# ELU output of a fused attention and mixture-of-experts kernel: transposed on VectorE and through DRAM instead of on TensorE

## The chip, the cores and the metric

The kernel runs on one core of one Trainium2 chip. The metric is device time in microseconds (us), the median of several runs; all times in this document are in us unless marked ns. The engines are TensorE (PE; its weight loads stand apart as PEld), VectorE (DVE), ScalarE (ACT), GpSimd (POOL) and SyncE (SP), which here only issues DMAs.

## The reference: what is computed

Three layers in a row, all in fp32 on the inputs of the reference (the first layer's weights arrive as float64 and are narrowed on the chip):

```python
# 1: attention, 8 batches x 8 heads, 576 positions, head size 64, causal by blocks of 64
scores = (q @ k.T) / 8, masked by blocks;  attn = softmax(scores);  x = attn @ v      # x: 4608 x 512
# 2: a dense layer with ELU
h = x @ w_in                                  # 4608 x 2048
g = where(h > 0, h, exp(min(h, 0)) - 1)
x2 = g @ w_out                                # 4608 x 512
# 3: soft mixture of experts: 8 experts, 4 slots each
logits = x2 @ phi                             # 4608 x 32
d = softmax(logits over tokens);  slot_input = d.T @ x2
slot_out[e] = relu(slot_input[e] @ w1[e]) @ w2[e]    # w1, w2: 16 MB each
out = softmax(logits over slots) @ slot_out          # 4608 x 512
```

x2 itself is never formed: the kernel folds `w_out @ phi` into one matrix of 2048 x 32 (`WP`), takes the logits as `g @ WP`, and gathers `d.T @ g` over all tokens before it multiplies by `w_out`.

## The kernel before

**Tiling.** The 4608 tokens are 36 tiles of 128. The 64 heads are 32 pairs of heads, four pairs to a batch. For each tile the first layer is done in four *ranges* of 512 of the 2048 columns. In one range TensorE runs 12 matmuls of 128x512 (lines 613 to 615: high by high, high by low, low by high parts, four steps over the 512 inputs) into one of two PSUM banks; ACT takes the exponential (L618); DVE forms min(e,1)-1 (L620) and then max(e,h) (L623), which is `g` of 128 tokens x 512 columns, put into one of the `NG` = 6 slots of the buffer `G`.

**The part that is changed.** The logits need `g` turned, with its 2048 columns on the partitions. So after each range `gtr` in `tile_range` turns it on TensorE in four 128x128 transposes (all transposes go by the helper on L312) into the PSUM bank `GTB`, and ACT or DVE copies that bank into `GT` (L288 or L290). `tile_logits` then multiplies each range by its 512 rows of `WP` (L636: four matmuls, recorded as eight, with 32 stationary and 128 moving columns; four column groups side by side). When all four ranges are in, `tile_dispatch` does the two softmaxes' steps (L648 to L676) and `d.T @ g` (L686), and adds that to a running sum (L690).

**Attention** uses the same engines between the ranges: block scores (L474, L478), row maxima and exponentials (L487, L490), normalisation on POOL (L507), 26 transposes a pair on TensorE (also L312), their copies (L288, L290), and the products with v (L573, L581). Its q and k are loaded in stripes of 32 partitions with runs of 128 bytes and turned by DVE (L443).

**Order.** The kernel is one static program. Each step is an operation with an engine, an estimated duration and a key; `Plan.order` simulates the engines and takes, on each of them, the operation with the lowest key among those whose inputs are ready by its estimate (for a DMA: issue, 0.65, bytes at 360 GB/s, and 1.0 more). Every engine, SP's queue too, runs its list in that order and waits at the head where an input is late. Tile i has key 22 i; the last attention pair is keyed at tile 30.

**Head and end.** Until some 160 us the float64 weights are loaded, narrowed and split while the first pairs of heads run. The expert weights and `w_out` (36 pieces of 1 MB, `piece` and `quarters` in `tail`, lines 749 and 763) have no buffers of their own: 24 slots become free one after the other, 12 in the attention's buffers, two in the ring `XR`, eight in the first layer's weights (two to a range), one in `XH`/`XL` and one in `GT`. The last two tiles run range by range together (`last_tiles`). After them come `slot_input` (L806), the experts (L827, L849), two rounds of four experts each, and the output (L916).

Of the kernel before, what the change touches and what calls it, by code (L numbers as in the profile page):

```python
# [27 lines left out]
NEV, NQ = 16, 1  # L28
TICK, DUTY, FILL, FN = 3.4, 0.5, 0.055, 128
# [21 lines left out]
class Plan:  # L51
# [9 lines left out]
    def __init__(self):  # L61
        self.ops = []
        self.writers = {}
        self.readers = {}
        self.fills = []
        self.load = {}

# [5 lines left out]
    def add(self, engs, dur, fn, r=(), w=(), key=0.0, nbytes=0, load=1.0):  # L73
# [17 lines left out]
        self.load[i] = load  # L91
        return i

    def order(self):
# [32 lines left out]
        while events:  # L127
            now = events[0][0]
            while events and events[0][0] <= now + 1e-9:
                _, kind, i = heapq.heappop(events)  # L130
                if kind == 0:
                    for e in self.ops[i][0]:
                        heapq.heappush(heaps[e], (self.ops[i][4], i))
            for e in engines:
                if free[e] > now + 1e-9:
                    continue
                h = heaps[e]
                while h and done[h[0][1]]:
# [12 lines left out]
                _, i = heapq.heappop(h)  # L151
                done[i] = True
                engs, dur, fn, deps, key, nbytes = self.ops[i]
                d = dur[engs.index(e)]
                busy[e] += d
                free[e] = now + d
                fin = now + d
                if nbytes:
                    dma_free = max(dma_free, fin + 0.65) + nbytes / 360e3
                    fin = dma_free + 1.0  # L160
                finish[i] = fin
                if e == "PE":
                    recent.append((now, now + d, self.load[i]))
                seq.append((now, i, e))
                heapq.heappush(events, (free[e], 1, -1))
                if fin > free[e] or any(f_[2] == i for f_ in self.fills):
                    heapq.heappush(events, (fin, 1, -1))
                for o in out[i]:
                    hop = 0.0 if nbytes else self.HOPS.get((e, self.ops[o][0][0]), 0.0 if self.ops[o][0][0] == e else 0.15)
                    ready_at[o] = max(ready_at[o], fin + hop)  # L170
                    missing[o] -= 1
                    if not missing[o]:
                        release(o)
# [24 lines left out]
def attention_moe_kernel(ctx: ExitStack, tc, q, k, v, w_in, w_out, phi, w1, w2, consts, out):  # L198
# [18 lines left out]
    SM = base.take(160)  # L217
# [14 lines left out]
    PW = 3200  # L232
    PB = aa.take(2 * PW)
    PAD = aa.take(12 * PIECE - aa.size)
# [16 lines left out]
    wo_f32 = dpool.tile([FF, DM], F32, name="wo_f32")  # L251
    successors = {}
# [52 lines left out]
    def load(o, i, nbytes, r=(), w=(), key=0.0, eng="SP"):  # L305
# [3 lines left out]
        add(engs, tuple(0.48 if x == "SP" else 0.67 for x in engs), fn, r, w, key, nbytes)  # L309
# [11 lines left out]


    def start():
# [3 lines left out]
        def init(e):  # L327
            nc.vector.memset(f(ACC, 512), 0.0)
            nc.vector.memset(f(SM, 160), 0.0)
            nc.vector.memset(f(sum_col, 20), 1.0)  # L330
            nc.vector.memset(f(NMX, 2), 1e30)
# [3 lines left out]
        def zero(e):  # L335
            for s in range(2):
                nc.gpsimd.memset(f(PB + PW * s + S, 64), 0.0)
            for s in range(NV):
                nc.gpsimd.memset(f(V + 640 * s, 640, 64, P).rearrange("p (h x) -> p h x", h=2)[:, :, 256:320], 0.0)
# [6 lines left out]
               [(GT + 1024 * j, 512, [("gt", 2 * j), ("gt", 2 * j + 1)]) for j in range(2)] + \  # L346
# [60 lines left out]
        def give_back():  # L407
# [3 lines left out]
            handover(["c"], [("wot", 0), ("wot", 1)])  # L411
            handover([("e", 0), ("e", 1)] + [("xr", p, 1, j) for p in range(2) for j in range(2)], [("stage", 5)])
# [42 lines left out]

    def wide(x):
        return S if x == "b" else P * (x[0] + 1)

    def pair_scores(n, fill, key):
# [25 lines left out]
        for x in units:  # L485
# [5 lines left out]
                f(PB + PW * s + UNITS[x][1], wide(x)), pb(at(x), wide(x)), AF.Exp, bias=f(c, 1), scale=1.0,  # L491
                accum_out=f(sum_col + 9 * s + UNITS[x][0], 1)),
                r=keys(x) + [("nm", s, x)], w=[("p", x, s), ("sum", s, fill // 2)], key=key)

    def pair_weights(n, half, key):
# [9 lines left out]
        for x in units:  # L505
            p = PB + PW * s + UNITS[x][1]
            add("POOL", 0.2 + wide(x) / 1050, lambda e, x=x, p=p: nc.gpsimd.tensor_scalar(  # L507
                out=f(p, wide(x)), in0=f(p, wide(x)), scalar1=f(rs_col + 9 * s + UNITS[x][0], 1), scalar2=0.0,
                op0=ALU.mult, op1=ALU.add), r=[("rs", s, half)], w=[("p", x, s)], key=key)
# [26 lines left out]
        for gi, (blocks, outs) in enumerate(groups):  # L536
            tb, tk = (POST, "post") if gi % 2 and n < NPB else (PTB, "ptb")

            def tr(e, blocks=blocks, tb=tb):
                for j, (x, c) in enumerate(blocks):  # L540
                    transpose(pb(tb + P * j, P), f(PB + PW * s + UNITS[x][1] + P * c, P))
            add("PE", 0.02 + 0.108 * len(blocks), tr, r=[("p", x, s) for x in {b[0]: 0 for b in blocks}] + ["con"], w=[tk], key=key, load=0.0)
# [20 lines left out]
    def pair_values(n, key):  # L563
# [7 lines left out]
        def first(e):  # L571
            for h in range(2):
                mm(pb(PTB, 64, 64 * h, 64 * h + 64), lhsT=f(vs + 320 * h, D), rhs=f(pts[h], 64), start=True, stop=True)  # L573
        add("PE", 0.17, first, r=rd, w=["ptb"], key=key, load=0.25)
        add(*evict(n, 64), lambda e: copy(e, f(XR + RING * p + ring, 64), pb(PTB, 64)), r=["ptb"], w=[("xr", p, b % 2, 0)], key=key)
        for c in range(5):
            q0 = max(64, P * c)

            def pv(e, c=c, q0=q0):
# [3 lines left out]
            add("PE", 0.02 + (S - q0) / 603, pv, r=rd, w=["pvb"], key=key, load=0.25)  # L583
# [5 lines left out]
    tslot = [(GT + 512 * j, ("gt", j)) for j in range(4)]  # L589
# [15 lines left out]
    def tile_range(i, r, hb, gs, ts, kr):  # L605
        s = i % 2
        xh, xl = XH + 512 * s, XL + 512 * s
        (g, gk), (gt, tk) = gs, ts
# [17 lines left out]

        def gtr(e):
# [3 lines left out]
        add(CP2, cpdur(512), lambda e: copy(e, f(gt, 512), pb(GTB, 512)), r=["gtb"], w=[tk], key=kr)  # L631

    def tile_logits(r, ts, bank, bk, kp):
# [4 lines left out]
        add("PE", 0.3, lg, r=["wp", ts[1]], w=[bk], key=kp, load=0.25)  # L638
# [55 lines left out]
    def moe_tile(i, key):  # L694
        gs = [gslot[(4 * i + r) % NG] for r in range(4)]
        tile_split(i, key - 6)
        for r in range(4):
            tile_range(i, r, r % 2, gs[r], tslot[r], key + 5.5 * r)
        for r in range(4):
            tile_logits(r, tslot[r], POST, "post", key + 17)  # L700
        tile_dispatch([i], [gs], [(POST, "post")], [(LPS, "lps")], (DTX, "dtx"), (DX, "dx"), key + 17)

    def last_tiles(i, key):

        order = [gslot[(4 * i + j) % NG] for j in range(NG)] + tslot[2:]
# [13 lines left out]
    def tail(key):  # L719
        att = [(nm, s, a) for nm in ("rq", "rk") for s in range(2) for a in range(4)] + [(nm, s) for nm in ("qt", "kt") for s in range(2)] + \  # L720
              [("v", s, j) for s in range(NV) for j in range(3)] + [("p", x, s) for x in UNITS for s in range(2)] + \
# [15 lines left out]
        slots += [(held("xhl", 0), hk), (lambda: f(GT, PIECE).rearrange("p (c d) -> p c d", d=512), [("gt", r) for r in range(4)])]  # L737
        for j, (_, olds) in enumerate(slots):
            handover([("piece", j, c) for c in range(4)], olds)
        turn = 2 * list(range(len(slots)))  # L740

        def piece(src, kp, r=()):
# [8 lines left out]
            add("SP", 0.48, fn, r, pkeys(j), kp, 1 << 20)  # L751
# [104 lines left out]
        def late(x, n, dtype, p0=0, p1=P):  # L856
            nm = "w3" if x < 2 * PIECE else "xhl"
# [4 lines left out]
        for m in range(9):  # L862
            handover([("cpkh", m)], sum((pkeys(j) for j in ((20, 21) if m < 8 else (22,))), []))
        handover([("sop", 0), ("sop", 1)], pkeys(22))
# [38 lines left out]
        places = [p1[1, g][1] for g in range(4)] + [23]  # L903
# [79 lines left out]
```

## Time and profile before

| | us |
|---|---|
| median of 3 runs | 1084.82 (1082.36 to 1086.9) |
| the profiled execution's own time | 1082.45 |
| its span, first to last instruction | 1080.7 |
| PE busy | 1034.6 (96%) |
| DVE busy | 617.5 (57%) |
| ACT busy | 499.5 (46%) |
| POOL busy | 275.6 (26%) |

Matmuls are pipelined, so the duration of one (its mean in ns) is longer than the time from one to the next; the chain of waits, which gives each piece of time to one instruction only, shows the latter. In the chain's rows the numbers are the start, the time that the piece adds, the engine, the tensor, the line and the count of instructions. In a table of stretches an engine's number is its busy time, with the count of instructions in brackets; the last three columns are the granted TensorE clock as a share of the full one, the mean busy share of the 16 DMA engines, and GB/s.

### The profile page before, as it was taken

To read this page: it belongs to the slowest core of one execution; us is meant where nothing else is said; L and a number is where in the kernel's file an instruction comes from. 1 tells how busy PE (TensorE), PEld (TensorE's weight loads), DVE (VectorE), ACT (ScalarE), POOL (GpSimd) and SP (SyncE) were. 2 spreads that over 40 slices of the span, in tenths; PEclk is the share of its full clock that TensorE was granted. 3 is DMA by queue.
4 is the path that set the end of the run, shared out by engine and by line. 5 is a ranking of instruction groups with operands and counts; after the bars stand their busy time and mean duration, and the time that the engine had idled before them with its cause. 6 is when DMAs were issued, how large, how long until landed. Compare 5 with 4: busy or idle time off the path is not lost.

```text
span 1080.7 us, 19505 instructions
## 1 busy us (share of the span) xinstructions
PE 1034.6 (96%) x7287; PEld 687.0 (64%) x7287; DVE 617.5 (57%) x1560; ACT 499.5 (46%) x1346; POOL 275.6 (26%) x396
## 2 busy tenths in 40 slices
PE   7878999999999999999999999999999999999993
PEld 4546676666666666666666666666766666767441
DVE  6989663455554555565756665656656564453241
ACT  3766453455454545454544534454444443332134
POOL 4886220122222313122323222231222222010000
PEclk9999889999999999999999999999999999999997
DMA  9988940011111111212111111121110024717969
GB/s 188 201 190 189 229 122 12 18 28 35 33 35 34 34 34 30 38 23 39 29 34 33 35 34 34 23 36 29 30 29 12 1 79 147 282 44 277 348 228 350
DMA packets 219486, 97.95 MB, mean 91 GB/s; under 512 B 192512, under 2 KB 192640, under 8 KB 219392
## 3 DMA queue, kind: packets, MB, share of 16 engines
q1 hardware_dynamic: 217616, 96.49, 34.4%
q8 instruction: 57, 0.93, 0.4%
q10 hardware_dynamic: 1776, 0.22, 0.2%
q14 instruction: 37, 0.30, 0.1%
HBM read 83.05 MB, written 13.63 MB: 89 GB/s over the span
## 4 chain that ended last, share of the span: by engine, by line
PE 86%; DMA 4%; DVE 3%; POOL 2%; SPq 1%; issue 1%; ACT 1%; ACTq 0%; DVEq 0%; POOLq 0%
PE ps L312 16%; PE ps L613 14%; PE ps L615 12%; PE ps L614 12%; PE ps L581 7%; PE ps L478 7%; PE ps L636 4%; PE ps L686 3%; PE ps L474 3%; PE ps L849 1%; POOL att L507 1%; PE ps L827 1%; SPq L307 1%; DMA wo_f<-att 1%; DVE att L374 1%; PE ps L652 1%
## 5 line engine op out<-in xcount | busy, mean ns | idle before, releaser
L613 PE MATMUL ps<-w,xhl 128*128 128x512 f32 x576 | 258.1, 448 | 0.0
L507 POOL TENSOR_SCALAR att<-att,base 128x128 f32<-128x128 f32 (+4 forms) x288 | 173.2, 619 | 246.8 <-DVE base L503 231.2
L615 PE MATMUL ps<-w,xhl 128*128 128x512 f32 x576 | 227.2, 394 | 0.4 <-POOL xhl L600 0.4
L614 PE MATMUL ps<-w,xhl 128*128 128x512 f32 x576 | 226.3, 393 | 0.0
L490 ACT ACTIVATE att<-ps,base 128x128 f32<-128x128 f32 (+4 forms) x288 | 157.4, 553 | 98.9 <-DVE base L487 94.6
L288 ACT COPY att<-ps 128x512 f32<-128x512 f32 (+3 forms) x217 | 106.1, 511 | 123.6 <-PE ps L312 119.0
L312 PE MATMUL ps<-base,att 128*128 128x128 f32 x864 | 140.9, 285 | 11.9 <-POOL att L507 7.4
L620 DVE TENSOR_SCALAR xe<-xe 128x512 f32<-128x512 f32 x144 | 67.6, 469 | 146.4 <-ACT xe L618 145.4
L487 DVE TENSOR_REDUCE base<-ps 128x1 f32<-128x128 f32 (+4 forms) x288 | 137.1, 506 | 23.4 <-PE ps L474 14.7
L312 PEld LDWEIGHTS ps<-base,att 128*128 128x128 f32 x864 | 102.4, 146 | 61.3 <-issue 22.7
L613 PEld LDWEIGHTS ps<-w,xhl 128*128 128x128 f32 x576 | 108.7, 189 | 48.9 <-issue 35.6
L618 ACT ACTIVATE xe<-ps 128x512 f32<-128x512 f32 x144 | 86.1, 598 | 88.5 <-PE ps L615 86.6
L615 PEld LDWEIGHTS ps<-w,xhl 128*128 128x128 f32 x576 | 108.2, 188 | 25.6 <-POOL xhl L600 0.9
L614 PEld LDWEIGHTS ps<-w,xhl 128*128 128x128 f32 x576 | 109.4, 190 | 10.1
L600 POOL TENSOR_TENSOR xhl<-xe,xhl 128x512 fp32r<-128x512 f32 x36 | 47.1, 1310 | 221.4 <-ACT xhl L598 187.7
L478 PE MATMUL ps<-att 64*128 64x128 f32 (+3 forms) x512 | 98.7, 478 | 4.8 <-ACT att L490 4.7
L623 DVE TENSOR_TENSOR g<-xe,ps 128x512 f32<-128x512 f32 x144 | 98.0, 680 | 3.3
L581 PE MATMUL ps<-att 128*64 128x512 f32 (+4 forms) x640 | 94.4, 427 | 0.0
L312 PE MATMUL ps<-base,g 128*128 128x128 f32 x592 | 90.3, 275 | 0.1
L288 ACT COPY g<-ps 128x512 f32<-128x512 f32 (+1 forms) x77 | 44.9, 584 | 87.0 <-PE ps L312 86.0
L312 PEld LDWEIGHTS ps<-base,g 128*128 128x128 f32 x592 | 70.1, 141 | 21.6 <-issue 4.9
L290 DVE COPY g<-ps 128x512 f32<-128x512 f32 (+1 forms) x77 | 52.5, 682 | 42.1 <-PE ps L312 41.5
(115 smaller groups left out, 1089.0 us busy)
## 6 DMA issues: line engine op xcount, KB each, us to landing
att<-in_moe_w_dram SPq DMA_DIRECT2D x12, 1024.0 KB, 13.7
att<-in_k_dram SPq DMA_DIRECT2D x127, 72.0 KB, 2.7
att<-in_q_dram SPq DMA_DIRECT2D x126, 72.0 KB, 2.6
att<-in_v_dram SPq DMA_DIRECT2D x64, 128.0 KB, 2.6
g<-in_moe_w_in_dram SPq DMA_DIRECT2D x16, 512.0 KB, 6.4
w_late<-in_moe_w_dram SPq DMA_DIRECT2D x8, 1024.0 KB, 6.6
att<-in_moe_w_dram SPq DMA_DIRECT2D x32, 256.0 KB, 5.8
out_dram<-att SPq DMA_DIRECT2D x16, 512.0 KB, 5.5
```

The source lines that it names most:

```text
L288: nc.scalar.copy(o, i)
L312: mm(o, lhsT=i, rhs=f(IDN + base, n, base, base + n), start=True, stop=True, is_transpose=True)
L478: mm(pb(at((u, h)), P * (u + 1)), lhsT=f(qt + P * u, P, 64 * h, 64 * h + 64), rhs=f(kt, P * (u + 1), 64 * h, 64 * h + 64), start=True, sto ...
L487: add("DVE", 0.08 + wide(x) / 960, lambda e, x=x, c=c: nc.vector.tensor_reduce(out=f(c, 1), in_=pb(at(x), wide(x)), axis=AX.X, op=ALU.max, ...
L490: add("ACT", 0.42 + wide(x) / 1300, lambda e, x=x, c=c: nc.scalar.activation(f(PB + PW * s + UNITS[x][1], wide(x)), pb(at(x), wide(x)), AF ...
L507: add("POOL", 0.2 + wide(x) / 1050, lambda e, x=x, p=p: nc.gpsimd.tensor_scalar(out=f(p, wide(x)), in0=f(p, wide(x)), scalar1=f(rs_col + 9 ...
L581: mm(pb(PVB + q0 - 64, S - q0, 64 * h, 64 * h + 64), lhsT=f(vs + 320 * h + D * c, D), rhs=f(pts[h] + CHS * c + q0, S - q0), start=(c == 0) ...
L613: mm(pb(bank, 512), lhsT=fr(xh + P * kk, P), rhs=hi, start=(kk == 0), stop=False)
L614: mm(pb(bank, 512), lhsT=fr(xh + P * kk, P), rhs=lo, start=False, stop=False)
L615: mm(pb(bank, 512), lhsT=fr(xl + P * kk, P), rhs=hi, start=False, stop=(kk == 3))
L618: add("ACT", 0.48, lambda e: nc.scalar.activation(f(ee, 512), pb(bank, 512), AF.Exp), r=[("h", hb)], w=[("e", hb)], key=kr)
L623: add("DVE", 0.6, lambda e: nc.vector.tensor_tensor(out=f(g, 512), in0=f(ee, 512), in1=pb(bank, 512), op=ALU.max), r=[("e", hb), ("h", hb) ...
```

## The change

For tiles 0 to 33 the transposes on TensorE, the bank `GTB` and the copies to `GT` go. DVE turns `g` by blocks of 32x32 into a new buffer `TT` (four blocks of rows stay where they were, each block turned in itself). For every two ranges (a half tile) SP writes 128 x 1024 words from `TT` to a DRAM tensor, waits for it, and reads it back in four loads of 32 partitions (runs of 1 KB), which puts the blocks in their places in `GT`. The logits of a tile become one operation behind both halves. The last two tiles keep the old way. `NG` becomes 8. The second half of a pair's weights is no longer double buffered (`PB`); attention's transposes alternate between two PSUM banks throughout, since `GTB` is free; the products with v become one operation. Expert weights have 22 slots, in another order, nine of them in the attention's buffers, and the first 12 pieces also wait in threes until the loads of tiles 30, 31, 32 and 33 have landed. The planner counts 2.5 instead of 1.0 behind the new DMAs.

```diff
+TLAG, PACE0, PACE = 2.5, 30, 3
-    NG = 6
+    NG = 8
     G = ga.take(NG * 512)
-    GT = ga.take(2048)
+    GT = ga.take(PIECE)
+    TT = ga.take(PIECE)
+    PAD = TT
-    PW = 3200
-    PB = aa.take(2 * PW)
-    PAD = aa.take(12 * PIECE - aa.size)
+    PW = (1664, 1536)
+    PB = aa.take(2 * PW[0] + PW[1])
...
+    def pat(x, n):
+        return PB + (PW[0] * (n % 2) + UNITS[x][1] if x in HALVES[0] else PW[0] + UNITS[x][1])
...
-            tb, tk = (POST, "post") if gi % 2 and n < NPB else (PTB, "ptb")
+            tb, tk = (PTB, "ptb") if gi % 2 == 0 else (POST, "post") if n < NPB else (GTB, "gtb")
...
     def tile_range(i, r, hb, gs, ts, kr):
...
+        if ts is None:
+
+            hf = r // 2
+            tt = f(TT + 1024 * hf, 1024).rearrange("p (b c j) -> p c b j", b=4, j=32)[:, 4 * (r % 2):4 * (r % 2) + 4]
+            add("DVE", 0.7, lambda e: nc.vector.transpose(out=tt, in_=f(g, 512).rearrange("p (c b i) -> p c b i", c=4, i=32)),
+                r=[gk], w=[("tt", hf, r % 2)], key=kr)
+            return
+
         def gtr(e):
...
+    def tile_turn(i, hf, kp):
+
+        via = turned[hf]
+        load(via, f(TT + 1024 * hf, 1024), 1 << 19, r=[("tt", hf, r) for r in range(2)], w=[("via", hf)], key=kp, lag=TLAG)
+        for b in range(4):
+            load(f(GT + 1024 * hf, 1024, 32 * b, 32 * b + 32).rearrange("i (a x) -> i a x", a=4),
+                 via.rearrange("(a i) (b x) -> b i a x", a=4, b=4)[b], 1 << 17, r=[("via", hf)],
+                 w=[("gt", hf, b)] + ([("turned", i)] if hf and b == 3 else []), key=kp, lag=TLAG)
+
+    def tile_routing(kp):
+        def lg(e):
+            for c in range(16):
+                j = c % 4
+                gt = f(GT + 1024 * (c // 8), 1024).rearrange("p (a c j) -> p c a j", a=4, j=32)[:, c % 8]
+                mm(pb(POST, P, 32 * j, 32 * j + 32), lhsT=f(WP + NS * c, NS), rhs=gt, start=(c < 4), stop=(c >= 12))
+        add("PE", 1.0, lg, r=["wp"] + gtk(0) + gtk(1), w=["post"], key=kp, load=0.25)
...
         for r in range(4):
-            tile_range(i, r, r % 2, gs[r], tslot[r], key + 5.5 * r)
-        for r in range(4):
-            tile_logits(r, tslot[r], POST, "post", key + 17)
+            tile_range(i, r, r % 2, gs[r], None, key + 5.5 * r)
+            if r % 2:
+                tile_turn(i, r // 2, key + 5.5 * r + 0.5)
+        tile_routing(key + 17)
...
-        slots = [(lambda j=j: f(PT + PIECE * j, PIECE).rearrange("p (c d) -> p c d", d=512), att) for j in range(12)]
-        slots += [(ring(hf), xk[hf]) for hf in range(2)]
-        slots += [(held("w%d" % r, j), wk[r]) for r in range(4) for j in range(2)]
...
+        wslot = [(held("w%d" % r, j), wk[r]) for r in range(4) for j in range(2)]
+        slots = [(flat(PT + PIECE * j), att) for j in range(9)]
+        slots += [(flat(TT), [("tt", j, r) for j in range(2) for r in range(2)])]
+        slots += wslot[:2] + [(ring(hf), xk[hf]) for hf in range(2)] + wslot[2:]
+        slots += [(held("xhl", 0), hk), (flat(GT), gtk(0) + gtk(1))]
...
-            add("SP", 0.48, fn, r, pkeys(j), kp, 1 << 20)
+            pieces.append(j)
+            paced = len(pieces) - 1
+            add("SP", 0.48, fn, list(r) + ([("turned", PACE0 + paced // PACE)] if paced // PACE + PACE0 < NTILE - 2 else []), pkeys(j), kp, 1 << 20)
```

## Rows read from the trace of the kernel before

**Rows 1.** The page: busy time of PE and DVE, and the slices.
```profile
PE 1034.6 (96%) x7287; PEld 687.0 (64%) x7287; DVE 617.5 (57%) x1560; ACT 499.5 (46%) x1346; POOL 275.6 (26%) x396
PE   7878999999999999999999999999999999999993
DMA  9988940011111111212111111121110024717969
```

**Rows 2.** The chain of waits from 300 to 400: shares by line.
```profile
by line: PE ps L312 19.4%; PE ps L613 16.9%; PE ps L615 14.4%; PE ps L614 14.3%; PE ps L581 11.0%; PE ps L478 8.3%; PE ps L636 5.1%; PE ps L474 4.5%; PE ps L686 4.0%; PE ps L573 1.1%; PE ps L652 0.9%; PE ps L653 0.6%
```

**Rows 3.** The chain from 938 to 956: one tile without attention.
```profile
938.42 0.99 PE ps L686 x8
...
940.31 0.44 PE ps L312 x4
...
945.33 0.57 PE ps L636 x16
945.90 0.43 PE ps L613
...
949.17 0.23 PE ps L613
...
949.87 0.36 PE ps L636 x8
...
954.90 0.99 PE ps L686 x8
```

**Rows 4.** Instructions of two TensorE lines; first and last start in us.
```profile
L312 PE MATMUL ps<-base,g 128*128 128x128 f32 x592 | 90.3, 275 | 0.1
L686 PE MATMUL ps<-g,base x272: 592/605/618, 172.8 to 971.8; 128*32 128x512 f32 x136
```

**Rows 5.** DVE and ACT groups, 200 to 880: busy, mean ns; idle time before.
```profile
L620 DVE TENSOR_SCALAR xe<-xe 128x512 f32<-128x512 f32 x109 | 52.0, 477 | 109.4 <-ACT xe L618 108.4
L290 DVE COPY g<-ps 128x512 f32<-128x512 f32 x55 | 37.6, 684 | 14.0 <-PE ps L312 13.4
L443 DVE STREAM_TRANSPOSE att<-att 128x576 f32<-128x576 f32 x46 | 34.8, 762 | 0.9 <-issue 0.8
L623 DVE TENSOR_TENSOR g<-xe,ps 128x512 f32<-128x512 f32 x109 | 74.0, 678 | 2.3
L618 ACT ACTIVATE xe<-ps 128x512 f32<-128x512 f32 x109 | 65.2, 598 | 55.2 <-PE ps L615 53.9
L288 ACT COPY g<-ps 128x512 f32<-128x512 f32 x53 | 31.1, 587 | 41.2 <-PE ps L312 40.8
```

**Rows 6.** DMA issues: count, KB each, median us from issue to landing.
```profile
att<-in_q_dram SPq DMA_DIRECT2D x126, 72.0 KB, 2.6
att<-in_v_dram SPq DMA_DIRECT2D x64, 128.0 KB, 2.6
wo_f<-att SPq DMA_DIRECT2D x16, 256.0 KB, 4.7
out_dram<-att SPq DMA_DIRECT2D x16, 512.0 KB, 5.5
```

**Rows 7.** Stretches: q and k loads alone, and the end's weights.
```profile
416.00:421.00 5.00, 5.00 (x41) 3.53 (x40) 4.07 (x11) 2.12 (x7) 3.66 (x7) 1.00 0.62 101
1010.00:1040.00 30.00, 29.88 (x280) 11.55 (x281) 6.74 (x11) 6.11 (x11) 0.00 (x0) 1.00 1.04 368
```

**Rows 8.** SP's queue: issues of q, 200 to 880 (ns); expert weights in order.
```profile
L307 SPq DMA_DIRECT2D att<-in_q_dram x84: 337/489/1382, 214.1 to 782.9; - x84
...
970.59 24.88 SPq L749 DMA_DIRECT2D w_late<-in_moe_w_dram  x8
...
1021.96 17.84 SPq L763 DMA_DIRECT2D att<-in_moe_w_dram  x16
```

**Rows 9.** The chain from 900 on: the end.
```profile
994.59 0.47 PE ps L636 x8
...
1043.77 2.09 PE ps L849 x7
```

More of the change, by code (lines that the diff above doesn't have):

```diff
@@ L251, in attention_moe_kernel @@
     wo_f32 = dpool.tile([FF, DM], F32, name="wo_f32")
+    turned = [dpool.tile([P, 1024], F32, name="turned%d" % j) for j in range(2)]
     successors = {}
@@ L308, in load @@
         engs = (eng,) if isinstance(eng, str) else eng
-        add(engs, tuple(0.48 if x == "SP" else 0.67 for x in engs), fn, r, w, key, nbytes)
+        add(engs, tuple(0.48 if x == "SP" else 0.67 for x in engs), fn, r, w, key, nbytes, lag=lag)
     def transpose(o, i, n=P, base=0):
@@ L320, in handover, with gtk @@
             plan.readers.setdefault(b, []).extend(sorted(ops))
+    def gtk(hf):
+        return [("gt", hf, b) for b in range(4)]
     def start():
@@ L345, in start @@
         raws = [(G + 1024 * j, 512, [("g", 2 * j), ("g", 2 * j + 1)]) for j in range(3)] + \
-               [(GT + 1024 * j, 512, [("gt", 2 * j), ("gt", 2 * j + 1)]) for j in range(2)] + \
+               [(GT + 1024 * j, 512, gtk(j)) for j in range(2)] + \
                [(XR + 2 * RING + S, RING, [("xr", p, 1, j) for p in (2, 3) for j in range(2)])]
@@ L411, in give_back @@
             handover(["c"], [("wot", 0), ("wot", 1)])
+            handover([("tt", 0, r) for r in range(2)], [("narrow", 0), ("narrow", 1)])
             handover([("e", 0), ("e", 1)] + [("xr", p, 1, j) for p in range(2) for j in range(2)], [("stage", 5)])
@@ L454, in attention_moe_kernel, with pkey @@
     HALVES = (FILLS[0] + FILLS[1], FILLS[2] + FILLS[3])
+    def pat(x, n):
+        return PB + (PW[0] * (n % 2) + UNITS[x][1] if x in HALVES[0] else PW[0] + UNITS[x][1])
+    def pkey(x, n):
+        return ("p", x, n % 2 if x in HALVES[0] else 0)
     def wide(x):
@@ L569, in pair_values, with pv @@
         ring = S * (b % 2)
-        def first(e):
+        def pv(e):
             for h in range(2):
                 mm(pb(PTB, 64, 64 * h, 64 * h + 64), lhsT=f(vs + 320 * h, D), rhs=f(pts[h], 64), start=True, stop=True)
[L574 to L579, printed above, removed]
+            for c in range(5):
+                q0 = max(64, P * c)
                 for h in range(2):
@@ L588, in attention_moe_kernel @@
     gslot = [(G + 512 * j, ("g", j)) for j in range(NG)]
-    tslot = [(GT + 512 * j, ("gt", j)) for j in range(4)]
+    tslot = [(GT + 512 * j, gtk(j // 2)) for j in range(4)]
     def tile_split(i, key):
@@ L720, in tail @@
         att = [(nm, s, a) for nm in ("rq", "rk") for s in range(2) for a in range(4)] + [(nm, s) for nm in ("qt", "kt") for s in range(2)] + \
-              [("v", s, j) for s in range(NV) for j in range(3)] + [("p", x, s) for x in UNITS for s in range(2)] + \
+              [("v", s, j) for s in range(NV) for j in range(3)] + [pkey(x, s) for x in UNITS for s in range(2)] + \
               [x for s in range(NPT) for x in pt_keys[s]]
@@ L733, in ring, with flat @@
             return lambda: f(XR, 4 * RING).rearrange("p (c t) -> p c t", t=RING)[:, :, S * hf:S * hf + 512]
-        slots = [(lambda j=j: f(PT + PIECE * j, PIECE).rearrange("p (c d) -> p c d", d=512), att) for j in range(12)]
-        slots += [(ring(hf), xk[hf]) for hf in range(2)]
-        slots += [(held("w%d" % r, j), wk[r]) for r in range(4) for j in range(2)]
-        slots += [(held("xhl", 0), hk), (lambda: f(GT, PIECE).rearrange("p (c d) -> p c d", d=512), [("gt", r) for r in range(4)])]
+        def flat(o):
+            return lambda: f(o, PIECE).rearrange("p (c d) -> p c d", d=512)
+        wslot = [(held("w%d" % r, j), wk[r]) for r in range(4) for j in range(2)]
[3 more added lines that the diff above has]
+        slots += [(held("xhl", 0), hk), (flat(GT), gtk(0) + gtk(1))]
         for j, (_, olds) in enumerate(slots):
@@ L740, in tail @@
         turn = 2 * list(range(len(slots)))
+        pieces = []
         def piece(src, kp, r=()):
@@ L856, in late @@
         def late(x, n, dtype, p0=0, p1=P):
-            nm = "w3" if x < 2 * PIECE else "xhl"
+            nm = "w2" if x < 2 * PIECE else "xhl"
             t = renew(nm, F32R, 1)
@@ L862, in tail @@
         for m in range(9):
-            handover([("cpkh", m)], sum((pkeys(j) for j in ((20, 21) if m < 8 else (22,))), []))
-        handover([("sop", 0), ("sop", 1)], pkeys(22))
+            handover([("cpkh", m)], sum((pkeys(j) for j in ((16, 17) if m < 8 else (20,))), []))
+        handover([("sop", 0), ("sop", 1)], pkeys(20))
         for s in range(2):
@@ L902, in tail @@
                 op0=ALU.mult, op1=ALU.add), r=[bk[2 * hf], "con"], w=[("sop", hf)], key=ko)
-        places = [p1[1, g][1] for g in range(4)] + [23]
+        places = [p1[1, g][1] for g in range(4)] + [14]
         NO = len(places)
```

37 lines of the change are left out of this document (20 added, 17 removed).

## Prediction

> **What bounds the kernel now.** I read four views: the page's busy times and slices, the chain of waits in the middle, the chain over one late tile, and the end. On the page TensorE is busy for 96% of the span, and from the seventh slice to the last but two it is busy throughout, while VectorE stands at 57% and the DMA engines at one to two tenths [rows 1]. A busy TensorE alone proves little, since durations overlap, so the chain decides: from 300 to 400 every piece of it is a TensorE line, and no wait on another engine or a DMA appears [rows 2]. There the kernel is as long as TensorE's list of work. A change that takes work off that list is worth the time which the chain gives to that work, as long as nothing else becomes late. The period of a tile is (971.8 - 172.8)/33 = 24.2 over the whole run [rows 4] and 954.90 - 938.42 = 16.48 where attention has ended [rows 3]. At the end another limit comes near: from 1010 to 1040 the DMA engines are at a share of 1.04 with 368 GB/s [rows 7], while TensorE is still in the chain.
>
> **What goes: the transposes.** 34 tiles x 4 ranges = 136 groups of four, 544 of the 592 in that row. The profile offers two prices. The mean of one is 275 ns [rows 4], which would make 150; but these overlap, and the chain gives a group of four 0.44 (940.31 to the next matmul) [rows 3]. I take the chain's: 136 x 0.44 = 59.8. The least I can defend is 0.39 a group (where a group stands next to other fp32 work, a part of the switch remains), so 53.
>
> **What goes: blocks of logits.** Matmuls, weights and columns stay the same in number; what changes is that one block of 32 recorded instructions takes the place of several. In the late tile the blocks are 0.57 for 16 and 0.36 for 8 (there are two of 8), 1.29 together; the second eight in a block cost 0.57 - 0.36 = 0.21, so 32 in one block cost 0.36 + 3 x 0.21 = 1.0, a gain of 0.3. Besides, the first matmul of the dense layer after such a block takes 0.43 [rows 3], about 0.2 more than its steady 0.23, and two of three such changes go: 0.4. That is 0.7 for a late tile. In the middle the share of 5.1% of 100 over 4.1 tiles is 1.2 a tile [rows 2], gain 0.2, and a block often stands beside other fp32 work. From 0 to 0.7 x 34 = 24; I take 0.35 x 34 = 12. The moving operand is now read in four runs of 32 words; no row shows that form, and I put its cost at nothing because the columns and their count are the same; were it half as slow again, 0.5 x 34 = 17 would go back.
>
> **What comes on VectorE.** A turn of 128x576 takes 762 ns [rows 5], so 512 columns take about 677: 136 x 0.68 = 92. The copies to `GT` were shared, 55 on DVE at 684 ns and 53 on ACT at 587 in 680 us [rows 5]; of 136 about 69 leave DVE (47) and 67 leave ACT (39). Net DVE gets 45 more, 662 of some 1025, or 65%. Its cover is the wait it has now: before L620 it idles 109.4 for ACT's exponential [rows 5]. I cost this at nothing; without the cover the price would be the 45.
>
> **What comes on the DMA engines.** Each tile writes 1.05 MB and reads 1.05 MB. At 368 GB/s [rows 7] that is 5.7 of a tile's 22, a quarter of the engines, on top of the tenth or two [rows 1]. The writes have 4 KB runs. Reads of 1 KB runs into 32 partitions are not in the trace; the nearest rows are the weights (368 GB/s) and the q and k loads, also 32 partitions but with 128-byte runs: 101 GB/s at a share of 0.62, so 163 at a full one [rows 7]. The reads take 2.9 to 6.4 a tile, nearer the former by their run length. In the middle both fit.
> The Trainium skill says against this form that a DMA into partitions 0 to 31 reaches only half of the SBUF ports and measured 189 GB/s at 1 MiB against 328 for 128 partitions (SBUF — State Buffer, "Door 1: The DMA port swizzle"). By it the reads of a tile would take 5.5, an estimate from that page, and the sum would change only at the end, where the engines are full (the rival on the end below). The row above, 163 at a full share, lies below that page's figure and can't tell it from the cost of short runs.
>
> **What comes on SP.** Ten issues a tile at 0.49 [rows 8] are 5 of 22. But SP waits at the head of its list, for the turn before a write and for the write before the four loads. Behind it stand q, k and v of the next pairs, which are loaded a tile and more ahead, and the next half's write. So it costs nothing while a round trip is a few us.
>
> **The new loop.** Logits now wait for the round trip, and TensorE meanwhile has the next tile's matmuls, up to the point where `G` has no free slot: range 0 of tile i+2 needs the `d.T @ g` of tile i. From the first range of tile i to that point: three ranges, then exponential 0.60, min 0.48, max 0.68, turn 0.68 [rows 5] (2.4), the round trip, logits 1.0, the softmax steps about 5.0 (949.87 to 954.90, with other work of TensorE between) and the product 0.99 [rows 3]. The round trip lies between 2.6 + 2.6 (128 KB loads, not held up) and 5.5 + 5.5 (512 KB in a full stretch) [rows 6]; I take 9. With attention: 16.5 + 2.4 + 9 + 7 = 35 against two periods of 22, 44: 9 to spare, no loss. Without it (tiles 30 on): the period would be 16.48 - 1.76 - 0.7 = 14.0, and 10.5 + 2.4 + 9 + 7 = 29 against 28, so half a us a tile, and more where the paced weights stand in the way. I take +4 for the last six tiles (0 to 10).
>
> **What moves: the expert weights.** Before, 22 pieces had been issued when the dense layer ended at 994.59 + 0.47 (eight of them from 970.59 to 995.5) [rows 8, 9], the last quarters are issued until 1039.8, and the last expert matmuls stand at 1043.77, 49 after the dense layer's end. Now nine pieces go into attention's space behind tiles 30 to 32, and the tenth waits for tile 33, some 11.5 into the 29 of the last two tiles (2.4 + 9), so 17 before the dense layer's end. With the two ring pieces ahead of it 25 are left: 25 x 1.05/0.368 = 71, so they end 54 behind the dense layer instead of 49. In tile 33, 5 pieces and 2.1 MB of turns (7.3 MB, 20 us) would have to fit into 14, so up to 6 more. I take +7 (0 to +15).
>
> **The rest.** Single buffers for half of the pair's weights, a third bank for attention's transposes, merged products, the head with its two moved staging areas: no row shows a gain or a loss. Bounds -5 to +20, taken as +4.
>
> **Sum** against the profiled execution's own 1082.45: -59.8 - 12 + 4 + 7 + 4 = -56.8, so 1025.7. The median of the runs shown is 1084.82, 2.4 above it; on that footing 1028. With the ends: 1084.8 - 60 - 24 - 5 = 996, and 1084.8 - 53 + 17 + 10 + 15 + 20 = 1094, all of them at once.
>
> **Rivals.**
> *The round trip holds TensorE (slower).* Place: the eight slots of `G`. For: each hop is a DMA with a landing time, and SP does them in turn with q, k and v. It decides from a loop of 44 on, a round trip of 18, and makes the kernel slower from a loop of 2 x 24.2 = 48.4, a round trip of 22; at 24, with 25 us a tile, 34 x 0.9 = 30 more than before: 1115. Against: the longest median of a transfer up to 512 KB is 5.5 [rows 6]. Chance 0.07.
> *The end is bound by DMA.* Reads at the q loads' 163 GB/s take 6.4 instead of 2.9, in the last four tiles 14 in all, where the engines have no room; the experts' last pieces are late by as much: 1028 + 14 = 1042, up to 1060. For: the share of 1.04 [rows 7]. Against: it needs all of it to be backlog. The skill's port rule (SBUF — State Buffer, as above) would do the same thing with 4 x 2.6 = 10. Chance 0.18.
> *VectorE sets the pace.* At 65% with more operations between an exponential and the release of a bank it answers late; all 45 of its net work would come back: 1073, half of it: 1050. For: L623 follows L620 at once [rows 5]. Against: 109 us of idle time before L620. Chance 0.08.
> *The turns don't unload TensorE.* The static order puts the logits where the estimate has them, and TensorE waits for what it saved: within 0.5% of 1085. Against: a step of three matmuls takes 3 x 0.23 = 0.69 [rows 3] where the planner counts 0.65, so TensorE runs behind the estimate and inputs come early for it. Chance 0.04.
> *More is saved,* the upper ends of the logits and no stall: 1000 to 1012. Chance 0.08.
>
> **How the numbers follow.** The forecast has 0.55, its own range is 1012 to 1042. With most of the end rival, half of VectorE's and of the larger gain the range is 1008 to 1060. Half a per cent (5.4) is about what a measurement of this kernel can tell from no change. Faster: 0.55 + 0.18 + 0.08 + 0.08 = 0.89; within 0.04; slower 0.07.
>
> **What would show it.** The L312 group from `g` falls from 592 to 48; the chain in the middle stays all TensorE; a late tile lasts about 14, one with attention about 22. The loads from the DRAM tensor land 4 to 5 after issue. DVE has 136 turns at about 0.68 and stands at 65%. From the dense layer's end to the end of the span it takes about 93 instead of 86. Wrong would be: idle time of TensorE before the logits or a chain through DMA in the middle (the loop), a chain through L620 and L623 (VectorE), or more than 65 between the dense layer's end and the last expert matmul (the end).

## The result and the profile after

The changed kernel takes 1044.3 (median of four runs, 1042.8 to 1047.1) against 1084.9: a ratio of 0.963, 95% interval 0.960 to 0.966. The direction was right, the size was not: 56.8 were forecast, 40.6 came. 1044.3 lies inside the wide range (1008 to 1060) and 2 above the forecast's own (1012 to 1042). The profiled execution is the longest of the four (1047.07, span 1045.3, so 35.4 below the span before); the positions below are its.

The page after: busy time, then slices of 26 each.

```profile
PE 973.0 (93%) x6822; PEld 649.2 (62%) x6822; DVE 644.9 (62%) x1603; ACT 465.7 (45%) x1302; POOL 278.5 (27%) x397
...
PE   7879889999999999999999999999999998669993
...
PEclk8989989999999999999999999999999999878996
DMA  9987845454545544545454444544532259875969
```

Against [rows 1], TensorE has lost 62 us of work and VectorE has gained 27. From the seventh slice to the thirty-third TensorE is still busy throughout. What is new stands in slices 34 to 36: an 8 and two 6, with DMA at 9, 8 and 7 and a lower granted clock (8, 7 and 8) in slices 35 to 37. The middle, as the chain of waits from 300 to 400 shows it (share by line; L317 is the old L312, L668 the old L636, L626 to L628 the dense layer):

```profile
by line: PE ps L626 21.0%; PE ps L628 16.4%; PE ps L627 16.4%; PE ps L317 11.1%; PE ps L593 10.4%; PE ps L494 10.0%; PE ps L490 4.5%; PE ps L668 4.0%; PE ps L724 4.0%; PE ps L589 1.1%; PE ps L690 0.9%; PE ps L691 0.6%; issue 0.0%
```

It is all TensorE as in [rows 2]: the transposes' line falls from 19.4% to 11.1%, and the dense layer's three rise from 45.6% to 53.8%, which is what more tiles in the same time look like. The groups of instructions (count | busy, mean ns | idle before), TensorE over the run, then VectorE from 200 to 880; and of the page the new DMAs (count, KB, us to landing):

```profile
L668 PE MATMUL ps<-g,base 128*32 128x128 f32 x1088 | 38.0, 280 | 10.7 <-DMA g<-turned 10.7
L317 PE MATMUL ps<-base,g 128*128 128x128 f32 x112 | 20.8, 315 | 4.4 <-DVE g L382 2.9 <-DVE g L636 1.5
```
```profile
L644 DVE STREAM_TRANSPOSE g<-g 128x512 f32<-128x512 f32 x121 | 83.3, 689 | 1.0
L633 DVE TENSOR_SCALAR xe<-xe 128x512 f32<-128x512 f32 x122 | 57.6, 472 | 75.7 <-ACT xe L631 74.9
```
```profile
turned<-g SPq DMA_DIRECT2D x68, 512.0 KB, 2.8
g<-turned SPq DMA_DIRECT2D x272, 128.0 KB, 3.0
```

The 592 of [rows 4] are 112: 48 of the last two tiles and the end, and 64 of the second layer's weights, whose staging now lies in this buffer. A turn takes 689 ns (677 forecast), and VectorE still waits 75.7 for ScalarE, 109.4 before [rows 5]. The median landing of write and load is 3, nearer the lower bounds of [rows 6].

**Where the gain was lost.** I counted the dense layer's matmuls (its last line, sixteen to a tile) in both traces:

| position | before | after | difference |
|---|---|---|---|
| first of the 31st tile | 892.8 | 832.8 | -60.0 |
| first of the 34th tile | 946.4 | 878.9 | -67.5 |
| last (dense layer's end) | 994.2 | 955.6 | -38.6 |
| end of the span | 1080.7 | 1045.3 | -35.4 |

Up to the 34th tile all that was forecast is there. The last three tiles' matmuls then take 76.7 instead of 47.8, and 29 are lost in that one stretch. Its chain of waits after (start, us, what; SPq and POOLq are the sequencers that issue):

```profile
895.18 0.47 issue
895.65 1.34 POOLq L1023
897.01 0.39 SPq L792
897.44 0.51 SPq L312
...
897.99 7.12 DMA g<-turned
...
914.49 0.43 PE ps L626
914.91 0.43 PE ps L627
...
921.93 0.24 PE ps L628
922.18 0.39 SPq L792
922.62 0.51 SPq L792
...
923.22 0.45 SPq L312
...
925.04 10.37 DMA g<-turned
```

Two things are to be seen. The loads of the turned halves land after 7 and 10 us instead of 3. And ahead of them in SP's list stand pieces of expert weights (L792): one for the ring `XR` at 897.01, which waits for the last use of the ring (on POOL), and two for the first layer's weight buffers at 922.18, which wait for TensorE's matmul of 921.93. SP's own list shows it (start, us from the first to the last issue, count), and below it SP's longest waits from 878 to 956 (who waited for whom: us, times, longest):

```profile
897.01 0.39 SPq L792 DMA_DIRECT2D xe<-in_moe_w_dram  x1
897.44 0.98 SPq L312 DMA_DIRECT2D g<-turned  x2
898.59 0.40 SPq L312 DMA_DIRECT2D turned<-g  x1
899.02 2.18 SPq L792 DMA_DIRECT2D att<-in_moe_w_dram  x3
905.19 0.34 SPq L312 DMA_DIRECT2D turned<-g  x1
906.35 1.76 SPq L312 DMA_DIRECT2D g<-turned  x4
922.18 0.94 SPq L792 DMA_DIRECT2D w_late<-in_moe_w_dram  x2
923.22 2.26 SPq L312 DMA_DIRECT2D g<-turned  x4
```
```profile
SPq L792 <- PE ps L628: 15.4, 2, 13.3
SPq L312 <- DMA turned<-g: 8.4, 2, 7.7
```

The last half was written from 905.19 on, and its four loads are issued at 923.22. Between them TensorE ran matmuls of the last two tiles. The chain gives 0.43 instead of 0.23 to the first 10 of them (0.41 to the next): after TensorE's idle time the granted clock had fallen towards the lower of its two levels, 0.55 in the mean from 910 to 920. Stretches after (the last three numbers: granted clock, DMA share, GB/s), the whole stretch from the 34th tile on among them, and the same work before, 946 to 994.6:

```profile
878.90:956.00 77.10, 57.83 (x342) 39.01 (x340) 22.35 (x50) 14.04 (x35) 2.58 (x2) 0.80 0.73 247
...
910.00:920.00 10.00, 8.53 (x28) 5.57 (x29) 1.94 (x3) 0.57 (x1) 0.00 (x0) 0.55 0.61 208
...
930.00:940.00 10.00, 3.42 (x25) 2.41 (x25) 0.99 (x5) 1.26 (x6) 0.00 (x0) 0.63 1.06 342
```
```profile
946.00:994.60 48.60, 48.57 (x315) 33.94 (x316) 19.94 (x43) 13.63 (x31) 2.71 (x2) 1.00 0.43 149
```

So the 29 have two parts: TensorE idles for 77.1 - 57.8 = 19.3, and it is busy for 57.8 instead of 48.6, 9 more, at a mean clock of 0.80 instead of 1.00. The second is an estimate of what the clock cost, since the two stretches don't hold quite the same instructions (342 and 315).

### The profile page after: what moved, and what is told of

It is laid out like the page before. It is cut to its first block, busy times and chain, and to the rows that moved or that the text cites. A ratio compares the mean times of both kernels' runs of the same rounds, so it can differ in the third digit from the quotient of the medians.

```text
span 1045.3 us, 19077 instructions
## 1 busy us (share of the span) xinstructions
PE 973.0 (93%) x6822; PEld 649.2 (62%) x6822; DVE 644.9 (62%) x1603; ACT 465.7 (45%) x1302; POOL 278.5 (27%) x397
## 4 chain that ended last, share of the span: by engine, by line
PE 80%; DMA 8%; DVE 4%; SPq 2%; POOL 2%; ACT 2%; issue 2%; POOLq 0%; ACTq 0%; DVEq 0%
PE ps L626 14%; PE ps L628 12%; PE ps L627 12%; PE ps L317 10%; PE ps L593 7%; PE ps L494 7%; PE ps L724 4%; PE ps L668 3%; PE ps L490 3%; SPq L312 2%; DMA g<-turned 2%; PE ps L894 1%; DMA wo_f<-g 1%; DMA g<-in_moe_w_out_dram 1%; POOL att L523 1%
## 5 line engine op out<-in xcount | busy, mean ns | idle before, releaser
L626 PE MATMUL ps<-w,xhl 128*128 128x512 f32 x576 | 251.9, 437 | 5.4 <-DVE g L636 4.7
L628 PE MATMUL ps<-w,xhl 128*128 128x512 f32 x576 | 228.5, 397 | 0.0
L293 ACT COPY att<-ps 128x512 f32<-128x512 f32 (+3 forms) x242 | 112.7, 510 | 111.9 <-PE ps L317 108.5
L626 PEld LDWEIGHTS ps<-w,xhl 128*128 128x128 f32 x576 | 110.2, 191 | 64.4 <-issue 31.6
L317 PE MATMUL ps<-base,att 128*128 128x128 f32 x800 | 118.4, 282 | 12.6 <-POOL att L523 8.7
L628 PEld LDWEIGHTS ps<-w,xhl 128*128 128x128 f32 x576 | 109.6, 190 | 25.2
L627 PEld LDWEIGHTS ps<-w,xhl 128*128 128x128 f32 x576 | 110.4, 192 | 14.2
L317 PEld LDWEIGHTS ps<-base,att 128*128 128x128 f32 x800 | 92.4, 144 | 43.0 <-POOL att L523 20.0
L636 DVE TENSOR_TENSOR g<-xe,ps 128x512 f32<-128x512 f32 x144 | 97.0, 676 | 2.4
L644 DVE STREAM_TRANSPOSE g<-g 128x512 f32<-128x512 f32 x136 | 93.6, 690 | 3.8 <-PE ps L317 2.7
L593 PE MATMUL ps<-att 128*64 128x512 f32 (+4 forms) x640 | 88.3, 422 | 0.0
L454 POOL TENSOR_SCALAR att<-att 128x576 f32<-128x576 f32 x32 | 23.4, 731 | 191.6 <-DVE att L452 163.5
L494 PEld LDWEIGHTS ps<-att 64*128 64x128 f32 x512 | 44.4, 194 | 40.6 <-issue 17.0
L593 PEld LDWEIGHTS ps<-att 128*64 128x64 f32 x640 | 43.3, 138 | 42.4 <-issue 33.1
```

The costliest lines, as they stand in the source:

```text
L293: nc.scalar.copy(o, i)
L317: mm(o, lhsT=i, rhs=f(IDN + base, n, base, base + n), start=True, stop=True, is_transpose=True)
L494: mm(pb(at((u, h)), P * (u + 1)), lhsT=f(qt + P * u, P, 64 * h, 64 * h + 64), rhs=f(kt, P * (u + 1), 64 * h, 64 * h + 64), start=True, sto ...
L593: mm(pb(PVB + q0 - 64, S - q0, 64 * h, 64 * h + 64), lhsT=f(vs + 320 * h + D * c, D), rhs=f(pts[h] + CHS * c + q0, S - q0), start=(c == 0) ...
L626: mm(pb(bank, 512), lhsT=fr(xh + P * kk, P), rhs=hi, start=(kk == 0), stop=False)
L627: mm(pb(bank, 512), lhsT=fr(xh + P * kk, P), rhs=lo, start=False, stop=False)
```

## The experiments

In the edits of e1, e2 and e5 only the part of a line is shown that says what a piece of weights waits for besides its space. Theory A: the turns' bytes stand behind those of the threes of weight pieces in the DMA engines. Theory B: their issues stand behind weight pieces in SP's list that wait for space. Ratios are to the kernel before, with 95% intervals. "End" is the dense layer's last matmul.

**e1, the pieces that wait for space held back**

```diff
...
-([("turned", PACE0 + paced // PACE)] if paced // PACE + PACE0 < NTILE - 2 else [])
+([("turned", PACE0 + paced // PACE if paced < 9 else NTILE - 3)] if paced < 16 else [])
...
```

> The changed kernel, but pieces 9 to 15 (the buffer TT, W0, the ring XR, W1) all wait for tile 33's loads; before, the ring's and W1's (12 to 15) waited only for their space. The burst of three pieces behind tiles 30, 31 and 32 stays. Theory A (the turns of tiles 31 to 33 stand behind the weights' bytes in the DMA engines): nothing much changes, their loads still take about 10 us to land, the step from tile 32's product to tile 33's stays near 30 us, total 1038 to 1046. Theory B (SP's list: a piece that waits for its space stands ahead of the turn's loads): SP's wait of some 15 us ahead of tile 33's last loads goes, the step falls below 20, total 1026 to 1032.

1032.9, ratio 0.952 (0.950 to 0.954). The step from tile 32's product to tile 33's is 19.7 instead of 30.4, the end at 937.9 instead of 955.6. Holding these four back is worth 18 at the end, and 11 in all. But the landing of the turns is still slow, 6.2 in the median from 855 to 945, so B isn't all. The total is just above B's 1026 to 1032.

**e2, all weights held back**

```diff
...
-([("turned", PACE0 + paced // PACE)] if paced // PACE + PACE0 < NTILE - 2 else [])
+([("turned", NTILE - 3)] if paced < 16 else [])
...
```

> The changed kernel, but no expert weight at all is loaded before tile 33's loads have landed. Both theories A and B: tiles 31 to 33 follow each other in 14 to 16 us, loads land in 3 us. If they still take over 18, neither is the cause but the loop through the eight slots itself. The price comes behind it: 36 MB in some 100 us from about 17 us before the dense layer's end, so from that end to the last expert matmul 85 us instead of 57, total 1043 to 1055.

1037.9, ratio 0.956 (0.954 to 0.959), better than expected. Steps of 12.8, 17.0 and 14.2 between the products of tiles 30 to 33, 14.7 in the mean, end at 923.9. With loads that land in 3 the loop through the eight slots is then no cause: it allows nearly the 14 that was forecast. The price is behind the end, 112 to the end of the span instead of 90, where the chain of waits goes through the weights' DMAs. Landing times of all DMAs on the DRAM tensor from 855 to 945, in the kernel after, then e1, then e2:

```profile
DMA to landing us min/median/max: 2.6/9.6/11.3
```
```profile
DMA to landing us min/median/max: 2.6/6.2/10.6
```
```profile
DMA to landing us min/median/max: 2.5/3.0/4.8
```

**e5, the fourth cell: waits for space, but no threes**

```diff
...
-([("turned", PACE0 + paced // PACE)] if paced // PACE + PACE0 < NTILE - 2 else [])
+([("turned", NTILE - 3)] if paced < 12 else [])
...
```

> The changed kernel with the threes of pieces (0 to 11) held until tile 33's loads have landed, while the ring's and W1's pieces (12 to 15) still go as soon as their space is free, and so may stand in SP's list ahead of a turn's loads: the fourth cell beside the changed kernel (both, dense layer's end at 955.6), e1 (threes only, 937.9) and e2 (neither, 923.9). If the two losses are independent, the end is at 940 to 943 and the total about 1043. If the list's wait comes only of turns that are late already, 924 to 930. If the list's wait is all, over 950.

1040.8, ratio 0.959 (0.956 to 0.962). End at 926.0, where it was expected if the list's wait comes only of turns that are late already; landing 3.1 in the median. The four cells, end of the dense layer:

| | no threes during tiles 31 to 33 | threes |
|---|---|---|
| ring and W1 pieces held | 923.9 (e2) | 937.9 (e1) |
| ring and W1 pieces free | 926.0 (e5) | 955.6 (after) |

The threes alone cost 14.0, the free pieces alone 2.1, both together 31.7, so 15.6 of it goes with the two together: neither A nor B alone. But the cells differ in one thing more. The planner makes the lists of SP and TensorE anew in each kernel, and it counts the threes' bytes.

In SP's list of the changed kernel the two W1 pieces stand ahead of the last half's four loads, and the longest of SP's waits above, 13.3, lies there. In e5 they stand behind them, and the loads are issued 6.4 after their write. So e5 doesn't show what W1 pieces ahead of turns that are on time would cost. An estimate from its rows: behind the pieces, which go at 907.37, the loads would have been issued some 6 later. That the late turns then make this wait longer (TensorE waits for the loads, W1's space for TensorE, the loads for W1's space) fits 13.3 against 6, but how the 15.6 divides between late turns and the order of the list was not run.

In TensorE's list e1 and the changed kernel have 48 matmuls of the dense layer ahead of the logits of tile 32, which is four ranges, and none between those logits and the product; e2 and e5 have 45 ahead and 15 between. In e1 TensorE no longer waits for a DMA from 876 to 938. It idles behind the logits, first for the softmax steps and then for the `max` that needs a freed slot. So the threes act there by way of the slots: the turns that the planner counts late, and that are late, leave TensorE nothing else to do.

Issues of e5 (as in SP's list above):

```profile
895.77 0.36 SPq L312 DMA_DIRECT2D turned<-g  x1
902.20 1.73 SPq L312 DMA_DIRECT2D g<-turned  x4
907.37 0.95 SPq L792 DMA_DIRECT2D w_late<-in_moe_w_dram  x2
```

**e3, the late tiles by TensorE**

```diff
...
+    NT0 = 30
...
-            tile_range(i, r, r % 2, gs[r], None, key + 5.5 * r)
-            if r % 2:
+            tile_range(i, r, r % 2, gs[r], tslot[r] if i >= NT0 else None, key + 5.5 * r)
+            if r % 2 and i < NT0:
                 tile_turn(i, r // 2, key + 5.5 * r + 0.5)
...
-            add("SP", 0.48, fn, list(r) + ([("turned", PACE0 + paced // PACE)] if paced // PACE + PACE0 < NTILE - 2 else []), pkeys(j), kp, 1 << 20)
+            add("SP", 0.48, fn, r, pkeys(j), kp, 1 << 20)
...
```

> Tiles 30 to 33 go the old way, by TensorE, and the expert weights are let go as soon as their space is free; tiles 0 to 29 as changed. Both theories: no wait for a turn behind tile 29, the late tiles take 16.5 us each as before the change, and from the dense layer's end to the end of the span 86 as before. Total 1028 to 1036. If the loss were in the head or in the middle, it would stay at 1040 or above.

1024.5, ratio 0.944 (0.941 to 0.947), 20 faster than the change itself and 4 better than expected. From tile 30 on a tile takes 16.5 to 17.2, the end is at 932.4, and 89.7 follow it.

**e8 and e10, how many tiles can go by DRAM before the weights must start**

Here the edit is shown against e3.

```diff
-    NT0 = 30
+    NT0 = 32
...
-            add("SP", 0.48, fn, r, pkeys(j), kp, 1 << 20)
+            add("SP", 0.48, fn, list(r) + ([("turned", NT0 - 1)] if paced < 16 else []), pkeys(j), kp, 1 << 20)
```

(e10: NT0 = 33.)

> As e3, but tiles 30 and 31 are turned by way of DRAM too, and pieces 0 to 15 wait for tile 31's loads; tiles 32 and 33 and the last two by TensorE. Two more tiles at 14 instead of 16.5, and the space for weights has idle time of the DMA engines to spare in e3: 1017 to 1022. If the later start of the weights shows at the end, 1025 or more.

> As e8 with one tile more by way of DRAM: tiles 0 to 32, pieces 0 to 15 behind tile 32's loads; tile 33 and the last two by TensorE. 2.5 less for that tile. If the space for the weights still has time to spare, 1018 to 1020; if they start too late for the experts, 1023 to 1032.

e8: 1021.5, ratio 0.941 (0.937 to 0.944), the fastest of all. Its end is at 930.1, and from there TensorE is at work while the DMA engines have little time to spare:

```profile
830.00:880.00 50.00, 48.25 (x330) 35.18 (x323) 27.49 (x61) 16.07 (x46) 7.02 (x9) 1.00 0.51 165
880.00:930.60 50.60, 50.58 (x349) 35.27 (x349) 21.05 (x46) 15.46 (x34) 2.83 (x2) 1.00 0.84 315
```

e10: 1029.7, ratio 0.949 (0.946 to 0.952). The dense layer ends 2.7 earlier (927.4), but 101 follow instead of 90: the weights started too late. The three tiles together bring the dense layer's end 5.0 forward (932.4 in e3 to 927.4), 1.7 a tile and not the 2.5 expected, and that counts only as long as the weights' start can slip.

**e4, logits in four operations**

```diff
-        add("PE", 1.0, lg, r=["wp"] + gtk(0) + gtk(1), w=["post"], key=kp, load=0.25)
...
+            add("PE", 0.3, lg, r=["wp"] + gtk(r // 2), w=["post"], key=kp, load=0.25)
```

> The changed kernel with a tile's logits in four operations, each behind its own half, instead of one. If one block of 32 is worth the 12 us of the forecast, this costs 8 to 14 against the changed kernel: 1052 to 1058. If the blocks cost nothing, 1042 to 1047.

1051.5, ratio 0.969 (0.966 to 0.971), between the two expectations, so the total alone doesn't decide. By tile 29's product it is only 1.4 behind (853.3 against 851.9). In the chain from 231.8 up to there, the logits have 5.0% of 621.5 = 31.1 instead of 4.4% of 620.2 = 27.3, so 0.14 a tile or 5 in 34 tiles. So one block is worth 1 to 5 and not the 12. Of the 7.2 between the medians, 4.1 stand between the two traces' spans, and most of that arose in the disturbed late tiles (steps of 26.7 and 28.1); the other 3 no trace shows.

**e9, the transposes kept beside the new way**

```diff
+            if i < 30:
+                def idle(e):
+                    for j in range(4):
+                        transpose(pb(GTB + P * j, P), f(g + P * j, P))
+                add("PE", 0.44, idle, r=[gk, "con"], w=["gtb"], key=kr, load=0.0)
```

> The changed kernel, where TensorE makes the four transposes of a range beside the new way in tiles 0 to 29 (120 groups, into the free bank, copied by nobody). What the removed groups were worth: at the chain's 0.44 a group, 53 by tile 29, so its product at 900 to 910 instead of 852 and a total of 1090 to 1100; at the 275 ns of one instruction, 132: 1170 or more; if they fitted into waits, under 20: at most 1065.

1100.9, ratio 1.014 (1.011 to 1.018): 56.6 above the change, so 0.47 for each of 120 groups, and tile 29's product is 59 late, 0.49. That is the chain's price (0.44 in [rows 3]) and a little more, and not the 4 x 275 = 1100 ns of [rows 4]. From 200 to 900 the instruction's own mean is still 277 ns:

```profile
L317 PE MATMUL ps<-base,g 128*128 128x128 f32 x448 | 68.8, 277 | 1.3 <-DVE g L636 0.8 <-ACT att L293 0.4
```

**e6, VectorE turns twice**

```diff
-            add("DVE", 0.7, lambda e: nc.vector.transpose(out=tt, in_=f(g, 512).rearrange("p (c b i) -> p c b i", c=4, i=32)),
-                r=[gk], w=[("tt", hf, r % 2)], key=kr)
+            for _ in range(2 if i < 30 else 1):
+                add("DVE", 0.7, lambda e: nc.vector.transpose(out=tt, in_=f(g, 512).rearrange("p (c b i) -> p c b i", c=4, i=32)),
+                    r=[gk], w=[("tt", hf, r % 2)], key=kr)
```

> The changed kernel, where VectorE turns each block row of tiles 0 to 29 twice into the same place (83 us more of VectorE). If VectorE's turns are hidden behind its waits for ScalarE, as forecast: tile 29's product within 5 us of 851.9, total at most 1052. If VectorE sets the pace: half or more of the 83 come back, total 1085 or more.

1043.7, ratio 0.962 (0.958 to 0.966): no difference from the change, with 120 more turns. Tile 29's product comes at 849.9. VectorE's busy time from 300 to 800 (third engine) rises from 338 to 392 in 500, and TensorE stays full:

```profile
300.00:800.00 500.00, 499.70 (x3435) 334.21 (x3432) 391.81 (x1001) 236.73 (x696) 139.84 (x215) 1.00 0.48 126
```

**e7, six slots of G**

```diff
-        gs = [gslot[(4 * i + r) % NG] for r in range(4)]
+        gs = [gslot[(4 * i + r) % 6] for r in range(4)]
...
-        order = [gslot[(4 * i + j) % NG] for j in range(NG)]
+        order = [gslot[j] for j in (6, 7, 4, 5, 0, 1, 2, 3)]
```

> The changed kernel with six instead of eight slots of G in tiles 0 to 33. The loop from a slot's filling to its release is, with the measured landing times, 16.5 + 2.4 + 7.5 + 7 = 33.4 in the middle, against 1.5 periods of 23 = 34.5 with six slots (two periods, 46, with eight). If the forecast's loop is right, the middle loses 0 to 1 a tile, total 1045 to 1075, and most of it in the late tiles (27.4 against 21). If the round trip costs nothing at all until much later, no change, 1040 to 1046. If the loop is longer than worked out, over 1080.

1073.9, ratio 0.989 (0.986 to 0.992): 29.6 slower than the change. By tile 29's product it is 22.6 late, 0.75 a tile, within what the loop's sum allowed. TensorE's longest wait is a matmul behind the `max` that fills the slot (waiter, waited for, us, times, longest; 200 to 850, e7, then the kernel after):

```profile
PE ps L626 <- DVE g L636: 9.4, 12, 2.2
```
```profile
PE ps L626 <- DVE g L636: 1.7, 3, 0.9
```

These are 7.7 more of waiting; in that stretch TensorE idles for 15.6 in all instead of 2.2, and the rest of the 22.6 is not idle time and was not separated. So the loop is real: with the new way, but without the two more slots, three quarters of the gain would be gone.

## Why the prediction was right in direction and short in size

**The transposes (59.8) and the blocks (12).** Their sum held: up to the 34th tile 132 x 0.44 + 33 x 0.35 - 4 = 65.6 were forecast and 67.5 came. Within it the transposes are somewhat larger (0.47 to 0.49 a group, e9) and merging the logits smaller (1 to 5, e4). Why a group is dearer than its own 0.44 was not separated; other matmuls and waits around it move too.

**VectorE at nothing.** Right, with room for as much again (e6). Its busy time rose by 27, not 45: the planner gave more of attention's copies to ScalarE (of those of 128x512 from 200 to 880, VectorE had 29 before and 19 after, ScalarE 67 and 81).

**The DMA engines in the middle.** Right. From 300 to 800 the share rises from 0.18 to 0.47 and the rate from 33 to 122 GB/s, so the turns move 89 GB/s for 0.29, some 307 at a full share: 2.1 MB take 6.8, and if the writes go at 368, the loads take 4.0 a tile, between the forecast's 2.9 and 6.4. The packets recorded in the trace after agree: from 300 to 800 those of 1 KB, which only the loads have, took 58 ns each in the mean, 281 GB/s on 16 engines, so 3.7 a tile.

```profile
300.00:800.00 500.00, 498.27 (x3400) 331.08 (x3399) 337.94 (x889) 239.16 (x705) 137.63 (x211) 1.00 0.47 122
```
```profile
300.00:800.00 500.00, 499.94 (x3456) 332.17 (x3455) 292.78 (x789) 242.24 (x677) 127.64 (x197) 1.00 0.18 33
```

The Trainium skill's figure for 32 partitions (SBUF — State Buffer, "Door 1: The DMA port swizzle"; 5.5 a tile by an estimate from it) is above that 4.0. No run here tests the figure on one load by itself: four follow each other, and a share counts the time of the engines alone. So it is neither borne out nor refuted.

**The loop, the step that failed.** "I take +4 for the last six tiles (0 to 10)", with 9 for a round trip. In the stretch from the 34th tile's first matmul to the dense layer's end the forecast had about +2 (the +4, less what tile 33 itself saves); it measured +28.9, some 19 of it idle time of TensorE and the rest matmuls at a lower clock. The round trip was not 9 but, with the last half, from 905.2 (write issued) to 935.4 (loads landed): 30. The prediction names the paced weights as standing in the way, but sizes them as bytes that end late: what is left of the +4, and up to 6 in the weights' term. Their cost falls on the turns between them, and the list of SP adds to it (e1, e2, e5). That the threes, with the lists planned for them, are at the root is shown: without them the end is at 923.9 or 926.0, with them at 937.9 or 955.6. How much the order of the lists has in it is not. The prediction did say that SP waits at the head of its list, but looked there only at q, k and v, in the middle; the weight pieces that the change leaves unpaced in the same list were not followed past the moved loads.

**The expert weights (+7).** The last expert matmuls stand 56.9 behind the dense layer's end instead of 49.6 (the row below against [rows 9]), which is the 7; behind them 4.1 came back, so the span's end is only 3.2 later against the dense layer's (86.5 to 89.7). It is no clean test, since the lost 29 gave the weights time; in e1, where the end is 17.7 earlier, 93.0 follow it, 6.5 more than before.

```profile
1012.49 1.12 PE ps L894 x8
```

The total lies where the rival on the end had it (1042 to 1060), but by another way: that the wide range held is in part luck. In e10 the late start of the weights does show at the end.

**The rivals.** The first rival, that the round trip holds TensorE, came true in the last tiles, with a sign that the prediction names for it: TensorE idles 10.7 before the logits of tiles 32 and 33 (the row of L668 above), and the chain goes through DMA there. The rival wanted a round trip of 18 with attention; the one of 30 is more than the eight slots cover, and with landings of 3 they cover it (e2). The forecast had looked for it with transfers of 5.5 that wait for nothing. In the middle it would have come with six slots (e7). The clock was no part of the prediction: 0.43 for a matmul instead of 0.23, at a granted 0.51 to 0.63, makes some 9 of the 29 lost, by the estimate above.

## What to carry to other kernels

Price work that goes off a full engine by what the chain gives it, not by the duration of one instruction; here the chain was right within some tenth (0.44 against 0.47 to 0.49). Where a DMA is put into a loop, follow every transfer that shares its queue list and its engines in the last stage too, and ask of each what it waits for: a list can hold a late transfer behind work that depends on it. And where bulk loads must start at a fixed point, end the latency-bound way a few tiles earlier (e8) rather than pace the loads between.

## What was not expected of the hardware

A round trip through DRAM of 512 KB out and four times 128 KB back had landings of 3.0 each in the median while the engines were half busy, and 9.6 from 855 to 945, with the weights' threes between them and the engines at a share of 0.6 to 1.06. TensorE's granted clock stood at 1.00 through the whole of 200 to 850 with the transposes gone, and fell to the lower of its two levels only after idle time in the last tiles (a mean of 0.55 from 910 to 920; in e2, where TensorE idles for 1.8 of the 47 from the 34th tile on, it stays at 1.00).
